# A fused attention and two-block feed-forward kernel: where four kinds of small steps run

## The chip, the cores and the metric

One core of a Trainium2 chip runs the whole program. The metric is the device time of one execution in microseconds (us). TensorE multiplies matrices into PSUM banks; VectorE, ScalarE and GpSimd do the elementwise work, each taking its instructions in a fixed order; SyncE (SP) issues the DMAs, in order too. VectorE is DVE in the rows, ScalarE ACT, GpSimd POOL, TensorE PE (PEld: its weight loads).

## The reference, cut to what matters

```python
def _attn_ref(q, k, v, g_q, g_k):              # q, k, v: (4, 12, 448, 64) float32
    def rmsnorm(x, g):
        rms = np.sqrt(np.mean(x * x, axis=-1, keepdims=True) + 1e-06)
        return x / rms * g
    q_n, k_n = rmsnorm(q, g_q), rmsnorm(k, g_k)
    scores = (1.0 / np.sqrt(64)) * np.matmul(q_n, k_n.transpose(0, 1, 3, 2))
    attn = np.exp(scores - np.max(scores, axis=-1, keepdims=True))
    attn = attn / (np.sum(attn, axis=-1, keepdims=True) + 1e-09)
    return np.matmul(attn, v).astype(np.float32)

x = attention output as 1792 x 768
x = (((x @ w1) * (x @ w2)) @ w3) @ w_out        # 768 -> 1024 -> 1024 -> 768
h = x @ w_in                                     # 768 -> 2048
return (h * np.clip(h + 3.0, 0.0, 6.0) / 6.0) @ w_out2
```

The attention inputs are float32. The six weight matrices are float64: they are scaled by a numpy float64 scalar.

## The kernel before, in words

All products with float32 accuracy are made of fp32r operands split into a high and a low part (`mm3`, lines 79 to 82: three matmuls per product). The low part is the source less the high part, made by a subtraction: of the weights and keys on GpSimd (`ws`, `woh`, `w`, `wis`, `wos`, `K`), of the query on VectorE (`qlo`).

The program has two large stages in time. In the first, 24 pairs of heads (NP = 24) go through attention, each in 8 steps: four 112-row blocks (NC = 4) of either head. A step t makes a score tile on TensorE (`score`, lines 536 and 537: query high and low part stacked on 128 partitions, against the key's high and low parts), scales it and takes its row maximum on VectorE (`scale_max`, L543), negates that maximum (`negate`, L550, one column of the 16-column tile `mx`), and takes the exponential on ScalarE one step later (`expo`, L555, with the negated maximum as bias and the row sum as second result). Eight steps later the probabilities are transposed on TensorE (L562), split by ScalarE (`thi`, L571) and VectorE (`tlo`, L581) and multiplied with V. The score tiles go through two PSUM banks.

Around it, a table of tasks (`at`, `tasks`, with the shifts of `SHIFT`) places the preparation of the next pairs by step: `qhi` at 8i, `qlo` at 8i+1, `ksplit` at 8i+6 (L516 on ScalarE, L517 on GpSimd), `load_q` and `load_k` of the pair after that, and for every second pair the norms of two pairs at once: squares (`ssq`, L436), sums (`ssum`, L442), then `rms1` and `rms2`, six small instructions on a 112 x 32 tile on VectorE (L448, L460 to L466) with a logarithm and an exponential on ScalarE between them. The query source tile `qr` has a single buffer, so its next load waits until the last reader is done. `xout` (L639, GpSimd) multiplies the attention output by the reciprocal row sums, which come back through DRAM as a broadcast.

Between the attention steps, `fill` puts matmuls of the feed-forward chain: first W' = w3 @ w_out (`wprime`), then, for each of four batches, w1 and w2 and W' (`layer1`, `layer2`). `Prep` converts the weights ahead of that: `convert` makes float32 bit patterns out of float64 words held as pairs of int32. Per weight tile, ScalarE scales the high word as a float (L135), VectorE shifts the low word right by 29 bits (L136), and two VectorE instructions join sign, exponent and mantissa (L138, L141).

In the second large stage the last block runs: its weights are converted by `conv_w` (the same `convert` on 128 x 768 tiles, two raw buffers `wr`; 13 of 32 before the stage's loop, 19 inside the first of its four rounds), split by `split` (L799 ScalarE, L800 GpSimd), and 36 matmuls per 128 columns of width follow, with the activation on ScalarE and VectorE (L871 to L876).

The order of instructions on an engine is made when the program is built: a planner takes them in the order of the program text and lets a later one go ahead where, by its own costs, the earlier one would not be ready.

Of the kernel before, what the change touches and what calls it, by code (L numbers as in the profile page):

```python
# [12 lines left out]
F32 = mybir.dt.float32  # L13
F32R = mybir.dt.float32r
I32 = mybir.dt.int32
SIGN = -(1 << 31)
AF = mybir.ActivationFunctionType
ALU = mybir.AluOpType
# [4 lines left out]
B, H, S, D = 4, 12, 448, 64  # L23
HP = H // 2
NP = B * HP
P = 128
# [20 lines left out]
def fused_kernel(ctx: ExitStack, tc: tile.TileContext, nat, qT, kT, vin, gq, gk,  # L47
                 w12, w3t, wo, win, wo2, outT):
    nc = tc.nc
# [15 lines left out]
    G = gs[:, 2:3]  # L65
# [3 lines left out]
    def fetch(pool, src, n, tag, bufs=2):  # L69
# [4 lines left out]
        else:  # L74
            r = pool.tile([P, n, 2], I32, tag=tag, bufs=bufs, name=tag)
            dma(r, src.bitcast(I32).rearrange("p (n t) -> p n t", t=2))
        return r
# [9 lines left out]
    def dma(out, src):  # L87
        return nc.sync.dma_start(out, src)
# [13 lines left out]
    def run_tasks():  # L102
        for fn, a in tasks.pop(now[0], ()):
            fn(*a)
# [24 lines left out]
    def convert(w, r):  # L129

        hi, lo = r[:, :, 1], r[:, :, 0]
        f = hi.bitcast(F32)
        nc.scalar.activation(f, f, AF.Copy, scale=2.0 ** -112)  # L135
        nc.vector.tensor_single_scalar(lo, lo, 29, op=ALU.logical_shift_right)  # L136
        yield 0.7
        nc.vector.scalar_tensor_tensor(out=lo, in0=hi, scalar=SIGN, in1=lo,  # L138
                                       op0=ALU.bitwise_and, op1=ALU.bitwise_or)
        yield 0.9  # L140
        nc.vector.scalar_tensor_tensor(out=w, in0=hi, scalar=3, in1=lo,  # L141
                                       op0=ALU.logical_shift_left, op1=ALU.bitwise_or)
        yield 0.9
# [258 lines left out]
    T = {}  # L402
    anchors = {}

    def attention(ap, rate):
# [10 lines left out]
                    dma(T["nat", i], nat[i].rearrange("p a b d -> p (a b) d"))  # L416

        def load_q(i):
            T["qr", i] = ap.tile([P, 2, S], F32, tag="qr", bufs=1, name="qr")
            dma(T["qr", i], qT[i])  # L420

        def load_k(i):
            T["kr", i] = ap.tile([P, 2, S], F32, tag="kr", bufs=1, name="kr")
# [14 lines left out]
        def ssum(i, g):  # L438
            x = T.pop(("nat", i))
            if i == g[0]:  # L440
                T["ss", g[0]] = ap.tile([CP, 2, len(g), 2 * NC], F32, tag="ss", bufs=2, name="ss")
            nc.vector.reduce_sum(T["ss", g[0]][:, :, i - g[0], :],  # L442
                                 x.rearrange("p (a b) d -> p a b d", a=2), axis=AX.X)

        def rms1(g):
            w = 16 * len(g)
            v = T["ss", g[0]].rearrange("p a b c -> p (a b c)")
            nc.vector.tensor_scalar(v, v, 1.0 / D, 1e-6, op0=ALU.mult, op1=ALU.add)  # L448
            y = ap.tile([CP, w], F32, tag="ry", bufs=2, name="ry")
            nc.scalar.activation(y, v, AF.Ln)  # L450
            nc.scalar.activation(y, y, AF.Exp, scale=-0.5)
            T["ry", g[0]] = y

        def rms2(g):
            n = len(g)
            w = 16 * n
            v = T.pop(("ss", g[0])).rearrange("p a b c -> p (a b c)")
            y = T.pop(("ry", g[0]))
            t = ap.tile([CP, w], F32, tag="rt", bufs=2, name="rt")
            nc.vector.tensor_mul(t, y, y)  # L460
            nc.vector.tensor_mul(t, t, v)
            nc.vector.tensor_scalar(t, t, -0.5, 1.5, op0=ALU.mult, op1=ALU.add)
            r = ap.tile([CP, w], F32, tag="rr", bufs=2, name="rr")
            nc.vector.tensor_mul(r, y, t)
            rq = ap.tile([CP, n, 8], F32, tag="rq", bufs=3, name="rq")
            nc.vector.tensor_scalar_mul(rq, r[:, : 8 * n].rearrange("p (a b) -> p a b", b=8), 0.125)  # L466
            for i in g:
                T["rq", i] = rq[:, i - g[0], :]
            T["rr", g[0]] = r
# [32 lines left out]

        def qhi(i):
            T["Q", i] = q = ap.tile([P, 2, S], F32R, tag="Q", bufs=2, name="Q")
            nc.scalar.activation(q, T["qr", i], AF.Copy, scale=G)

        def qlo(i):
            a = slice(64, 128)
            q = T["Q", i]
            nc.vector.scalar_tensor_tensor(out=q[a], in0=T["qr", i][a], scalar=G[a, :], in1=q[a],  # L510
                                           op0=ALU.mult, op1=ALU.subtract)

        def ksplit(i):
            k1, k2 = T["K", i] = [ap.tile([P, 2, S], F32R, tag=f"K{z}", bufs=2, name="K") for z in range(2)]
# [12 lines left out]
        def score(i, s):  # L527
            j, c = divmod(s, NC)
            if s == 0:
                T["PP", i] = ap.tile([CP, NC, 2 * S], F32, tag="PP", bufs=2, name="PP")  # L530
                T["m", i] = ap.tile([CP, 16], F32, tag="mx", bufs=2, name="mx")
                T["sum", i] = ap.tile([CP, 8], F32, tag="sum", bufs=2, name="sum")
            k1, k2 = T["K", i]
            ps = bank("s")
            qs = T["Q", i][:, j, c * CP : c * CP + CP]
            nc.tensor.matmul(ps[:CP, :S], qs, k1[:, j, :], start=True, stop=False)  # L536
            anchors[8 * i + s] = [nc.tensor.matmul(ps[:CP, :S], qs, k2[:, j, :], start=False, stop=True)]  # L537
            return ps
# [8 lines left out]

        def negate(i, s):
            m = T["m", i]
            nc.vector.tensor_scalar_mul(m[:, 8 + s : 9 + s], m[:, s : s + 1], -1.0)  # L550

        def expo(i, s):
            j, c = divmod(s, NC)
            v = T["PP", i][:, c, j * S : j * S + S]
            anchors[8 * i + s].append(nc.scalar.activation(  # L555
                v, v, AF.Exp, bias=T["m", i][:, 8 + s : 9 + s], accum_out=T["sum", i][:, s : s + 1]))
# [124 lines left out]
        for i in range(NP):  # L681
            t = 8 * i
            n = i + 1
# [9 lines left out]
            if i % 2 == 0 and i + 2 < NP:  # L693
                g = groups[i + 2]
# [19 lines left out]
            if i % 2 == 0 and i + 2 < NP:  # L714
                g = groups[i + 2]
# [5 lines left out]
        t = -1  # L721
        while t < 8 * NP + 22 or xs_ready:
            t += 1
            if t == 4:
                first.close()
            now[0] = t
            live = t < 8 * NP
            ps = score(*divmod(t, 8)) if live else None
            if 0 < t <= 8 * NP:
                expo(*divmod(t - 1, 8))  # L730
            u = t - LG
            if 0 <= u < 8 * NP and u % 8 < 7:
                trans(*divmod(u, 8))
            if 0 <= u - 1 < 8 * NP and (u - 1) % 8 < 7:
                tlo(*divmod(u - 1, 8))
            if live:
                scale_max(t // 8, t % 8, ps)
                negate(*divmod(t, 8))
            if 0 <= u < 8 * NP and u % 8 < 7:
                thi(*divmod(u, 8))  # L740
            if 0 <= u - 2 < 8 * NP and (u - 2) % 8 < 7:
                pv(*divmod(u - 2, 8))
            with ExitStack() as es:
                for a in anchors.get(t - (3 if "pool" in L else 2), ()):
                    es.enter_context(tc.issue_after(a.ins))
                fill(*rate(t))
            run_tasks()
            if "pool" in L:
                xnext()
# [37 lines left out]
    def conv_w(q):  # L787
# [4 lines left out]
        else:  # L792
            for _ in convert(wf[q].bitcast(I32), r):
                pass
# [10 lines left out]
    step, q = 0, 0  # L805
# [33 lines left out]
    for b, t in enumerate(order):  # L839
        acc = None  # L840
        for m in range(M2):
# [26 lines left out]
            if acc is None:  # L868
# [4 lines left out]
                                           op0=ALU.min, op1=ALU.mult)  # L873
            g = lp.tile([P, 2, S], F32R, tag="g", bufs=2, name="g")
# [57 lines left out]
```

## Time and profile before

| what | value |
|---|---|
| timed runs | 1273.02 us median of 3 (1271.57 to 1277.7) |
| profiled execution | 1276.18 us, of which 1274.3 us span from first to last instruction |
| granted TensorE clock, mean | 0.968 |
| TensorE busy | 1183.1 us, 93% |
| VectorE busy | 795.1 us, 62% |
| ScalarE busy | 678.8 us, 53% |
| GpSimd busy | 463.6 us, 36% |
| DMA moved | 203.72 MB |

The busy time of an engine is a share of the whole span; a stage in which another engine sets the pace shows only in a table by stretch. [...]

### The profile page before, as it was taken

What the parts mean: (1) busy time and instruction counts of PE and PEld (TensorE: products, weight loads), DVE (VectorE), ACT (ScalarE), POOL (GpSimd) and SP (SyncE); (2) the same over time, 40 slices, a digit from 0 to 9 for tenths busy, and PEclk for the clock granted to TensorE, in tenths of its full rate; (3) what the DMA queues carried; (4) which work ended last, traced back from release to release, by engine and by line L of the source; (5) the groups of instructions that cost most, each with busy time, mean ns of one, the idle gap of its engine ahead of it and who ended that gap; (6) DMA issues with size and microseconds to landing.
All of it is one profiled execution on the core that took longest, in us unless ns stands there. A gap on an engine that the chain in (4) does not pass through costs nothing.

```text
span 1274.3 us, 16884 instructions
## 1 busy us (share of the span) xinstructions
PE 1183.1 (93%) x5868; PEld 1033.9 (81%) x5868; DVE 795.1 (62%) x1524; ACT 678.8 (53%) x1305; POOL 463.6 (36%) x292
## 2 busy tenths in 40 slices
PE   3587998888889999999999999889999999999998
PEld 2355987667668999999998998778999999999997
DVE  6989789989993578768643446994433343343332
ACT  5887667866783566766642223444533353344332
POOL 4334324624443112222111003445454454545542
PEclk9698998989999999999999999899999999999999
DMA  7898664666688666676349983450100020001001
GB/s 248 253 256 243 202 193 167 194 229 228 211 274 306 209 217 199 235 225 220 134 163 382 348 323 113 158 173 25 60 28 1 1 87 1 1 1 44 1 1 44
DMA packets 64693, 203.72 MB, mean 160 GB/s; under 512 B 8544, under 2 KB 25440, under 8 KB 64608
## 3 DMA queue, kind: packets, MB, share of 16 engines
q1 hardware_dynamic: 64608, 202.65, 48.2%
q8 instruction: 46, 0.75, 0.2%
q14 instruction: 39, 0.32, 0.1%
HBM read 173.93 MB, written 28.68 MB: 159 GB/s over the span
## 4 chain that ended last, share of the span: by engine, by line
PE 67%; DMA 11%; DVE 10%; issue 5%; ACT 3%; POOL 2%; SPq 1%; DVEq 0%; POOLq 0%; ACTq 0%
PE bank L80 8%; PE bank L82 8%; PE bank L81 8%; PE acc L81 6%; PE acc L82 6%; PE acc L80 5%; PE h L80 5%; PE h L81 5%; PE h L82 5%; PE bank L562 3%; DMA raw<-in_w_dram 2%; DVE wf L141 2%; DMA wr<-in_wo_dram 2%; PE bank L536 2%; PE bank L537 2%
## 5 line engine op out<-in xcount | busy, mean ns | idle before, releaser
L800 POOL TENSOR_TENSOR wis<-wf,wis 128x768 fp32r<-128x768 f32 x63 | 119.8, 1902 | 234.1 <-ACT wis L799 234.1
L872 DVE SCALAR_TENSOR_TENSOR u<-u,h 128x448 f32<-128x448 f32 x64 | 39.5, 618 | 217.3 <-ACT u L871 217.3
L800 POOL TENSOR_TENSOR wos<-wf,wos 128x768 fp32r<-128x768 f32 x64 | 119.0, 1860 | 103.6 <-ACT wos L799 103.6
L80 PE MATMUL bank<-xhl,ws 128*128 128x448 f32 x384 | 145.1, 378 | 7.7 <-ACT ws L285 6.3
L543 DVE CUSTOM_DVE_ANT_0 PP<-bank,rb,rq 112x448 f32<-112x448 f32 x192 | 129.1, 677 | 31.9 <-PE bank L537 27.4
L82 PE MATMUL bank<-xhl,ws 128*128 128x448 f32 x384 | 143.9, 375 | 4.9 <-POOL ws L287 4.9
L81 PE MATMUL acc<-g,wos 128*128 128x448 f32 x384 | 144.3, 376 | 3.8 <-DVE g L876 3.7
L555 ACT ACTIVATE PP<-PP,mx 112x448 f32<-112x448 f32 x192 | 127.4, 664 | 37.4 <-DVE mx L550 34.2
L80 PE MATMUL acc<-g,wos 128*128 128x448 f32 x384 | 138.5, 371 | 5.5 <-ACT g L875 5.5
L82 PE MATMUL acc<-g,wos 128*128 128x448 f32 x384 | 143.2, 373 | 0.0
L81 PE MATMUL bank<-xhl,ws 128*128 128x448 f32 x384 | 142.5, 371 | 0.1
L80 PE MATMUL h<-x2h,wis 128*128 128x448 f32 x378 | 139.0, 368 | 0.0
L81 PE MATMUL h<-x2h,wis 128*128 128x448 f32 x378 | 138.9, 368 | 0.0
L82 PE MATMUL h<-x2h,wis 128*128 128x448 f32 x378 | 137.5, 364 | 0.4 <-POOL wis L800 0.4
L876 DVE TENSOR_TENSOR g<-u,g 128x448 fp32r<-128x448 f32 x64 | 97.9, 1529 | 33.6 <-ACT g L875 33.6
L871 ACT ACTIVATE u<-h,half 128x448 f32<-128x448 f32 x64 | 40.4, 631 | 143.2 <-PE h L82 143.2
L536 PE MATMUL bank<-K,Q 128*112 128x448 f32 x192 | 78.3, 409 | 37.5 <-DVE mx L543 25.0
L562 PE MATMUL bank<-ident,PP 112*128 112x112 f32 x672 | 97.0, 267 | 11.8 <-DVE xl L581 10.2
L562 PEld LDWEIGHTS bank<-ident,PP 112*128 112x128 f32 x672 | 80.5, 145 | 33.8 <-DVE xl L581 13.3
L571 ACT ACTIVATE xh<-bank 128x448 fp32r<-128x448 f32 (+1 forms) x156 | 83.0, 537 | 43.3 <-PE bank L562 38.4
L581 DVE TENSOR_TENSOR xl<-bank,xh 128x448 fp32r<-128x448 f32 x142 | 87.1, 615 | 25.5 <-ACT xh L571 23.8
L799 ACT ACTIVATE wos<-wf 128x768 fp32r<-128x768 f32 x64 | 54.1, 846 | 86.9 <-PE acc L82 86.7
(126 smaller groups left out, 2763.5 us busy)
## 6 DMA issues: line engine op xcount, KB each, us to landing
ws<-w12d SPq DMA_DIRECT2D x48, 768.0 KB, 5.1
ws<-wpd SPq DMA_DIRECT2D x32, 768.0 KB, 4.2
raw<-in_w_dram SPq DMA_DIRECT2D x32, 384.0 KB, 4.3
w12d<-ws SPq DMA_DIRECT2D x16, 768.0 KB, 6.0
wr<-in_win_dram SPq DMA_DIRECT2D x16, 768.0 KB, 4.5
wr<-in_wo_dram SPq DMA_DIRECT2D x16, 768.0 KB, 6.6
nat<-in_nat_dram SPq DMA_DIRECT2D x24, 448.0 KB, 5.9
qr<-in_qT_dram SPq DMA_DIRECT2D x24, 448.0 KB, 6.4
```

What stands on the lines that cost most here:

```text
L80: nc.tensor.matmul(ps, lh, rh, start=first, stop=False)
L81: nc.tensor.matmul(ps, lh, rl, start=False, stop=False)
L82: return nc.tensor.matmul(ps, ll, rh, start=False, stop=last)
L536: nc.tensor.matmul(ps[:CP, :S], qs, k1[:, j, :], start=True, stop=False)
L543: anchors[8 * i + s].append(nc.vector.tensor_tensor_reduce(out=T["PP", i][:, c, sl], in0=ps[:CP, :S], in1=T["rb", i][:, sl], op0=ALU.mult, ...
L555: anchors[8 * i + s].append(nc.scalar.activation(v, v, AF.Exp, bias=T["m", i][:, 8 + s : 9 + s], accum_out=T["sum", i][:, s : s + 1]))
L562: nc.tensor.transpose(ps[:, c * CP : c * CP + CP], src[:, c, kb * P : kb * P + P], ident[:CP, :CP])
L571: nc.scalar.activation(hi, ps, AF.Copy)
L581: nc.vector.tensor_sub(lo, ps, hi)
L799: nc.scalar.activation(t[:, 0, :], wf[q], AF.Copy)
L800: nc.gpsimd.tensor_sub(t[:, 1, :], wf[q], t[:, 0, :])
L876: nc.vector.tensor_sub(g[:, 1, :], u, g[:, 0, :])
```

## The change

Five edits. The shift of the low word becomes a ScalarE activation: it reads the upper 16 bits of the low word as an unsigned integer, multiplies by 2^-13, adds 2^-14 - 0.5 and writes an int32, which rounds to the top three bits. The norm steps of all groups but the first go to GpSimd. The query is loaded on 64 partitions instead of twice on 128; ScalarE scales it in place and copies it as the high part in a second instruction, and GpSimd subtracts to get the low part. Maxima are negated two columns at a time on odd steps. The exponential is placed one step later.

```diff
@@ convert
         hi, lo = r[:, :, 1], r[:, :, 0]
+        top = r.bitcast(U16).rearrange("p n (t s) -> p n t s", s=2)[:, :, 0, 1]
         f = hi.bitcast(F32)
         nc.scalar.activation(f, f, AF.Copy, scale=2.0 ** -112)
-        nc.vector.tensor_single_scalar(lo, lo, 29, op=ALU.logical_shift_right)
+        nc.scalar.activation(lo, top, AF.Copy, scale=2.0 ** -13, bias=2.0 ** -14 - 0.5)
@@ load_q
-            T["qr", i] = ap.tile([P, 2, S], F32, tag="qr", bufs=1, name="qr")
-            dma(T["qr", i], qT[i])
+            T["qr", i] = ap.tile([D, 2, S], F32, tag="qr", bufs=1, name="qr")
+            dma(T["qr", i], qT[i][:D])
@@ rms1, rms2
+        def eng(g):
+            return nc.gpsimd if g[0] else nc.vector
-            nc.vector.tensor_scalar(v, v, 1.0 / D, 1e-6, op0=ALU.mult, op1=ALU.add)
+            eng(g).tensor_scalar(v, v, 1.0 / D, 1e-6, op0=ALU.mult, op1=ALU.add)
...
-            nc.vector.tensor_mul(t, y, y)
+            eng(g).tensor_mul(t, y, y)
...
@@ qhi, qlo
-            nc.scalar.activation(q, T["qr", i], AF.Copy, scale=G)
+            qr = T["qr", i]
+            nc.scalar.activation(qr, qr, AF.Copy, scale=G[:D, :])
+            nc.scalar.activation(q[:D], qr, AF.Copy)
-            nc.vector.scalar_tensor_tensor(out=q[a], in0=T["qr", i][a], scalar=G[a, :], in1=q[a],
-                                           op0=ALU.mult, op1=ALU.subtract)
+            nc.gpsimd.tensor_sub(q[D:], T["qr", i], q[:D])
@@ negate
-            nc.vector.tensor_scalar_mul(m[:, 8 + s : 9 + s], m[:, s : s + 1], -1.0)
+            if s % 2:
+                nc.vector.tensor_scalar_mul(m[:, 7 + s : 9 + s], m[:, s - 1 : s + 1], -1.0)
@@ the step loop
-            if 0 < t <= 8 * NP:
-                expo(*divmod(t - 1, 8))
+            if 1 < t <= 8 * NP + 1:
+                expo(*divmod(t - 2, 8))
```

## Rows read from the trace of the kernel before

**Rows 1.** The page, part 1: busy us, share of the span, instructions.
```profile
PE 1183.1 (93%) x5868; PEld 1033.9 (81%) x5868; DVE 795.1 (62%) x1524; ACT 678.8 (53%) x1305; POOL 463.6 (36%) x292
```

**Rows 2.** Busy time of each engine by stretch; the first line names the columns.
```profile
core 0: us, PE busy (x) PEld busy (x) DVE busy (x) ACT busy (x) POOL busy (x), PEclk, DMA share, GB/s
0.00:400.00 400.00, 323.51 (x1553) 255.61 (x1554) 349.99 (x833) 287.25 (x619) 165.56 (x123) 0.91 0.73 228
400.00:650.00 250.00, 250.00 (x1383) 226.67 (x1382) 164.57 (x405) 151.31 (x326) 49.19 (x34) 1.00 0.63 207
...
785.00:870.00 85.00, 76.10 (x339) 65.66 (x337) 79.77 (x70) 37.81 (x54) 40.06 (x20) 0.94 0.40 140
```

**Rows 3.** The same view for 40 to 100 us, the same columns.
```profile
40.00:100.00 60.00, 44.67 (x186) 26.79 (x184) 56.32 (x133) 48.22 (x99) 24.74 (x18) 0.83 0.88 238
```

**Rows 4.** Waits of TensorE, 0 to 400 us: total us, times, longest.
```profile
PE bank L536 <- DVE mx L543: 25.0, 16, 5.8
...
PE bank L562 <- DVE xl L581: 10.2, 8, 3.3
```

**Rows 5.** Groups by line, VectorE, 0 to 400 us: count, busy us, mean ns, idle.
```profile
L510 DVE SCALAR_TENSOR_TENSOR Q<-qr,gs,Q 64x896 fp32r<-64x896 f32 x16 | 26.3, 1646 | 3.8 <-ACT Q L505 3.4
...
L136 DVE TENSOR_SCALAR raw<-raw 128x384 int32<-128x384 int32 x48 | 23.0, 480 | 10.5 <-DMA raw<-in_w_dram 5.6 <-DMA raw<-in_wo_dram 4.7
...
L550 DVE TENSOR_SCALAR mx<-mx 112x1 f32<-112x1 f32 x116 | 16.2, 143 | 0.5
...
L136 DVE TENSOR_SCALAR raw<-raw 128x512 int32<-128x512 int32 x16 | 11.8, 736 | 1.6 <-DMA raw<-in_w3t_dram 1.6
...
L460 DVE TENSOR_TENSOR rt<-ry 112x32 f32<-112x32 f32 x12 | 7.1, 590 | 0.1
L634 DVE TENSOR_SCALAR sum<-sum 112x8 f32<-112x8 f32 x14 | 5.4, 384 | 0.0
...
L464 DVE TENSOR_TENSOR rr<-ry,rt 112x32 f32<-112x32 f32 x10 | 2.3, 229 | 0.0
```

**Rows 6.** The same view, ScalarE and GpSimd.
```profile
L517 POOL TENSOR_TENSOR K<-kr,K 128x896 fp32r<-128x896 f32 x16 | 35.5, 2216 | 33.6 <-ACT K L516 26.7 <-DMA nat<-in_nat_dram 6.8
...
L135 ACT ACTIVATE raw<-raw 128x384 f32<-128x384 f32 x48 | 26.6, 556 | 13.9 <-DMA raw<-in_w_dram 11.5 <-DMA raw<-in_wo_dram 2.2
...
L505 ACT ACTIVATE Q<-qr,gs 128x896 fp32r<-128x896 f32 x16 | 16.6, 1034 | 1.9 <-DMA qr<-in_qT_dram 1.9
...
L639 POOL TENSOR_TENSOR xs<-xs,rsb 128x448 f32<-128x448 f32 x12 | 14.4, 1202 | 27.4 <-DMA rsb<-rsd 19.4 <-DVE raw L136 2.7 <-ACT PP L555 2.1
...
L135 ACT ACTIVATE raw<-raw 128x512 f32<-128x512 f32 x16 | 10.7, 670 | 3.8 <-DMA raw<-in_w3t_dram 3.7
```

**Rows 7.** Timeline, 817.9 to 827.6 us: start, us, engine, line, operation, tiles.
```profile
817.96 0.33 SPq L88 DMA_DIRECT2D wr<-in_win_dram  x1
...
822.39 0.55 DVE L136 TENSOR_SCALAR wr<-wr 128x768 int32<-128x768 int32 x1
...
822.44 0.94 ACT L135 ACTIVATE wr<-wr 128x768 f32<-128x768 f32 x1 [3.30 <-DMA wr<-in_win_dram]
...
823.28 0.56 ACT L875 ACTIVATE g<-u 128x448 fp32r<-128x448 f32 x1
...
823.41 0.96 DVE L138 SCALAR_TENSOR_TENSOR wr<-wr 128x768 int32<-128x768 int32 x1 [0.47 <-ACT wr L135]
...
824.83 2.60 DVE L141 SCALAR_TENSOR_TENSOR wf<-wr 128x768 int32<-128x768 int32 x1
...
827.49 0.33 SPq L88 DMA_DIRECT2D wr<-in_win_dram  x1
```

**Rows 8.** Stretch 40 to 100 us, L136 alone: busy (count), clock, DMA.
```profile
40.00:100.00 60.00, 6.51 (x13) 0.83 0.88 238
```

**Rows 9.** L550 and L634: count, duration ns least/median/most, first and last start.
```profile
L550 DVE TENSOR_SCALAR mx<-mx x192: 130/147/156, 22.4 to 640.4; 112x1 f32<-112x1 f32 x192
...
L634 DVE TENSOR_SCALAR sum<-sum x24: 151/172/1244, 44.9 to 641.4; 112x8 f32<-112x8 f32 x24
```

More of the change, by code (lines that the diff above doesn't have):

```diff
@@ L15 @@
 I32 = mybir.dt.int32
+U16 = mybir.dt.uint16
 SIGN = -(1 << 31)
@@ L459, in rms2 @@
             t = ap.tile([CP, w], F32, tag="rt", bufs=2, name="rt")
-            nc.vector.tensor_mul(t, y, y)
-            nc.vector.tensor_mul(t, t, v)
-            nc.vector.tensor_scalar(t, t, -0.5, 1.5, op0=ALU.mult, op1=ALU.add)
+            eng(g).tensor_mul(t, y, y)
+            eng(g).tensor_mul(t, t, v)
+            eng(g).tensor_scalar(t, t, -0.5, 1.5, op0=ALU.mult, op1=ALU.add)
             r = ap.tile([CP, w], F32, tag="rr", bufs=2, name="rr")
-            nc.vector.tensor_mul(r, y, t)
+            eng(g).tensor_mul(r, y, t)
             rq = ap.tile([CP, n, 8], F32, tag="rq", bufs=3, name="rq")
-            nc.vector.tensor_scalar_mul(rq, r[:, : 8 * n].rearrange("p (a b) -> p a b", b=8), 0.125)
+            eng(g).tensor_scalar_mul(rq, r[:, : 8 * n].rearrange("p (a b) -> p a b", b=8), 0.125)
             for i in g:
@@ L504, in qhi @@
             T["Q", i] = q = ap.tile([P, 2, S], F32R, tag="Q", bufs=2, name="Q")
-            nc.scalar.activation(q, T["qr", i], AF.Copy, scale=G)
+            qr = T["qr", i]
+            nc.scalar.activation(qr, qr, AF.Copy, scale=G[:D, :])
+            nc.scalar.activation(q[:D], qr, AF.Copy)
         def qlo(i):
-            a = slice(64, 128)
             q = T["Q", i]
-            nc.vector.scalar_tensor_tensor(out=q[a], in0=T["qr", i][a], scalar=G[a, :], in1=q[a],
-                                           op0=ALU.mult, op1=ALU.subtract)
+            nc.gpsimd.tensor_sub(q[D:], T["qr", i], q[:D])
         def ksplit(i):
```

## The prediction, made before the changed kernel was run

> **What bounds the kernel now.** I read the busy table first [rows 1]: TensorE 93%, VectorE 62%, ScalarE 53%, GpSimd 36%. It suggests TensorE, but these are averages over stages with different limits, so the second view is the same table by stretch [rows 2]. From 400 to 650 us TensorE is busy all the time, at full clock, and gets through 1383 matmuls, 5.53 per us. In the first 400 us it gets through 1553, for which that rate would need 281 us: 119 us are lost there, and that is the most that anything can win in this stretch. There VectorE is busy 350.0 of 400 us (0.875), ScalarE 287.3 (0.72), GpSimd 165.6 (0.41); in the densest part, 40 to 100 us, VectorE 56.3 of 60 (0.94) and ScalarE 48.2 (0.80) [rows 3]. The third view, TensorE's waits in these 400 us, names VectorE again: 25.0 us for the scaled maxima of L543, which give back the score bank, and 10.2 us for the low parts of L581 [rows 4]. So up to 400 us the bound is VectorE's queue; after that it is TensorE, except for one stretch: from 785 to 870 us TensorE loses 9 us, its clock is 0.94, and VectorE is busy 79.8 of 85 us [rows 2]. What is won or lost before 400 us reaches the end one to one, since TensorE has no slack to swallow it afterwards.
>
> **What VectorE loses, first 400 us.** The query low parts L510: 16 instructions, 26.3 us. The shift L136: 48 of 480 ns and 16 of 736 ns, 34.8 us. The norm steps: six groups of 10 to 12 small instructions, 24.1 us, of which L460 (7.1) is the largest and L464 (2.3) the smallest; the first of twelve pairs of heads stays on VectorE, so 22.1 us go. The negations L550: 116 of 143 ns, 16.2 us; half as many at the same price save 8.1 [rows 5]. Together 91 us: VectorE falls from 350 to 259 us.
>
> **What ScalarE gains.** The shift becomes an activation of the form of L135: same tile, same stride of 8 bytes, so I price it by L135's rows, 26.6 + 10.7 us. The query's second pass over 64 partitions has as many columns as L505, 16.6 us [rows 6]. That is 53.9 us of durations. Consecutive activations overlap: L135 starts at 822.44, lasts 0.94, and the next starts at 823.28 [rows 7], 0.10 early. Over 80 new ones this takes 8 us off: ScalarE goes from 287 to 333 us and becomes the fullest engine of the stage.
>
> **What GpSimd gains.** The query low part has the columns of L517, 2216 ns: 16 of them, 35.5 us. No norm step on GpSimd is in the trace. A line through L639 (448 columns, 1202 ns) and L517 (896 columns) [rows 6] puts 32 columns at 0.3 us; bounds are 0.2 (VectorE's own small price, L464, 229 ns) and 1.2 (L639). I take 0.3, about 65 instructions in the stretch: 20 us. GpSimd goes to 221 us, 0.55. What hides it: the low part is emitted at step 8i+1 and its first matmul at step 8i+8; 116 steps took 400 us (the count of L550, [rows 5]), 3.4 us each, so 24 us of cover for 2.2 us of work. The norm results run pairs ahead. If the cover is gone, 16 times 2.2 us, 35 us, is the price. Behind a waiting low part stand on GpSimd the key low parts, the split of V and the weight low parts; on SP the next load of q, which needs its single buffer back, and every load issued behind it.
>
> **The sum of this stage.** If ScalarE at 333 us is packed as tightly as VectorE was (0.875), the stage takes 381 us, 19 less. In 40 to 100 us nothing is won: 13 of the shifts there [rows 8] and two query passes bring ScalarE from 48 to about 56 of 60 us, where VectorE was. I take 3 us off for that: −16. Bounds: packed to VectorE's best 0.94 it is 354 us, −46; packed as ScalarE is now (0.72), 463 us, +63. I stand near the middle value because ScalarE's idle time is largely waiting on the VectorE queue that gets lighter, and because the exponential, emitted one step later, finds its maximum ready.
>
> **The negation in pairs.** The trace has a warning. L550, one element wide, took 130, 147 and at most 156 ns in 192 instructions; L634, the same operation eight wide, took 151, 172 and up to 1244 ns [rows 9], with a mean of 384 in the first 400 us [rows 5]. Something holds the wider one and never the narrow one. The change makes the narrow one two wide. The price is between zero and L634's excess over L550, 58 times 0.24 us, 14 us of VectorE; I take half as VectorE time, 7 us, and zero on the path, since 266 us is still far under ScalarE's 333.
> [...]
>
> **The weight conversion from 785 to 870 us.** One loop sets the pace there, visible in [rows 7]: the load of `wr` is issued at 817.96, lands for L135 at 822.44, L138 starts at 823.41 when L135 is done, L141 ends at 827.43, and the next load of that buffer goes out at 827.49: 9.53 us, about 9 such rounds in the stretch. L136 costs this loop nothing, it runs at 822.39 beside L135. Its successor runs after L135 on ScalarE and holds L138 0.84 us longer (822.44 to 823.28). TensorE's own 36 matmuls need less than the loop. Six of the nine rounds are paced by it, the first ones having their loads in hand: +5. Bounds: +8 if all nine are, and −10 if VectorE's queue, relieved of two L136 of 0.55 us per round, was the true limit.
>
> **Loads of q.** 448 KB become 224 KB, 16 times in the stretch. DMA was no releaser of TensorE there; bounds 0 and −4, I take −1.
>
> Sum: −16 + 5 − 1 = −12. The profiled execution took 1276.2 us (span 1274.3), so 1264; it lies 3.2 above the median of the timed runs, 1273.0, so the forecast is 1261 us. The likeliest case has a range of its own from 1245 to 1269.
>
> **Rivals.**
> 1. ScalarE cannot be filled. It is the engine that everything else releases: its order is fixed, and now the logarithm of the norm waits behind GpSimd (2.2 us key parts, and L639, which kept GpSimd 19.4 us waiting for its broadcast [rows 6]), and conversions need two activations where one did. Its best stretch so far is 0.80 [rows 3]. At 0.80 the stage takes 416 us: +16 + 5 − 1, 1293 us. It decides at 333/400 = 0.83: packed below that, the stage is slower than before. For: the added wait and the 0.72. Against: it idles on VectorE's results. Chance 0.20.
> 2. The paired negation is held behind GpSimd on the path: scaled maxima queue behind it, TensorE waits for the bank. 14 us come back: 1275 us, no change. For: L634. Against: VectorE's slack. Chance 0.13.
> 3. VectorE was the whole problem and ScalarE packs to 0.94 except for the densest part, with the clock returning as TensorE runs denser: half to two thirds of −46, near −30 + 4: 1247 us. For: [rows 4] lists hardly a wait on ScalarE of that size. Chance 0.14.
> The edits doing nothing because the removed work was hidden anyway is part of 2: it would show as a first stage of 400 us with an emptier VectorE.
> The forecast itself: 0.53.
>
> **How the numbers follow.** A change under 0.5% (6.4 us) can't be told from none here. Faster than that: 0.47 of the forecast's 0.53 and all of rival 3, 0.61. Within: 0.06 of the forecast, 0.09 of rival 2, 0.03 of rival 1, 0.18. Slower: 0.17 of rival 1 and 0.04 of rival 2, 0.21. The range goes from 1238, half of rival 3, to 1288, just short of rival 1.
>
> **What would show it.** In the first 400 us of work (116 steps): VectorE near 0.7, ScalarE near 0.87, fewer waits of TensorE on L543; L550's successor with a maximum far over 156 ns tells rival 2. Between 785 and 870 us: a round of 10.3 us instead of 9.5. The forecast is wrong if the point where TensorE becomes saturated does not move ahead by 10 us or more, or if ScalarE's waits on GpSimd grow by more than VectorE's shrink.

## The result and the profile after

The changed kernel took 1286.55 us (median of 4 runs, 1286.45 to 1288.95) against 1273.49 for the kernel before on the same chip: ratio 1.0105, 95% interval [1.0087, 1.0124]. It is 13 us slower; the forecast was 12 us faster. The profiled execution has a span of 1284.7 us.

The page's first part (busy us, share, instructions), to be read beside [rows 1]:

```profile
PE 1183.0 (92%) x5868; PEld 1034.1 (80%) x5868; DVE 729.0 (57%) x1242; ACT 747.0 (58%) x1425; POOL 530.2 (41%) x382
```

Work did move as the change says: VectorE lost 66 us over the run, ScalarE gained 68, GpSimd 67. TensorE does the same work in the same busy time, so the 10 us more of span are 10 us more in which it stands. The first two stretches of [rows 2] and the 85 us from the last stage's first activation, same columns:

```profile
0.00:400.00 400.00, 314.17 (x1486) 245.91 (x1487) 310.86 (x624) 320.72 (x687) 205.72 (x195) 0.89 0.69 210
400.00:650.00 250.00, 250.00 (x1375) 226.70 (x1374) 151.23 (x348) 155.29 (x335) 74.73 (x53) 1.00 0.64 207
...
798.40:883.40 85.00, 75.09 (x350) 64.57 (x351) 64.28 (x53) 52.33 (x74) 41.10 (x20) 1.00 0.41 140
```

The whole loss lies in the first line. TensorE gets through 1486 matmuls in place of 1553 and its granted clock (PEclk, a share of full speed) is 0.89 in place of 0.91; 314.2 x 0.89 against 323.5 x 0.91 is 15 us less of full-speed work. Some 9 us of that are TensorE standing longer (85.8 us against 76.5), the other 6 the lower granted clock. From 400 to 650 us it is saturated in both kernels, so the lag is carried: the last stage's first activation comes at 798.4 us where it came at 784.6 (+13.8). In the last stage 3.4 us are won back: from that first activation to the last 475.3 us, before 478.7. And no engine is full in the first 400 us: VectorE 0.78, ScalarE 0.80, GpSimd 0.51, TensorE 0.79. They wait for one another.

TensorE's waits in that stretch (line waited for, total us, times, longest), beside [rows 4]:

```profile
PE bank L541 <- POOL Q L516: 21.3, 2, 15.7
PE bank L568 <- DVE xl L587: 15.5, 10, 4.7
PE bank L541 <- DVE mx L548: 13.3, 16, 2.0
```

The wait for the scaled maxima was halved (25.0 to 13.3), as intended. The wait for the low parts grew from 10.2 to 15.5, and TensorE's first score now waits for GpSimd's low part, until 15.7 us where before it started at 11.4; the second of these two waits, 5.7 us, is at 54 us.

VectorE's groups by line and form in the first 400 us (busy us, mean ns), beside [rows 5]:

```profile
L143 DVE SCALAR_TENSOR_TENSOR raw<-raw 128x384 int32<-128x384 int32 x48 | 40.4, 843 | 0.5
L140 DVE SCALAR_TENSOR_TENSOR raw<-raw 128x384 int32<-128x384 int32 x48 | 40.0, 836 | 11.6 <-ACT raw L138 10.7 <-POOL K L522 0.9
...
L556 DVE TENSOR_SCALAR mx<-mx 112x2 f32<-112x2 f32 x57 | 23.1, 406 | 0.3
...
L640 DVE TENSOR_SCALAR sum<-sum 112x8 f32<-112x8 f32 x14 | 10.3, 738 | 4.3 <-ACT PP L561 4.2
```

Half as many negations take 23.1 us where 116 narrow ones took 16.2. The two joins of the 384-column tiles cost 836 and 843 ns where they cost 685 and 716, and L640 costs 738 where it cost 384. So of the 91 us that were taken off VectorE a good part returned as longer durations of what stayed: summed over all its groups, 403 us became 346, −57 and not −91. The difference is mostly the negation (23.1 us where 8.1 were forecast, +15.0), the joins of both widths (91.6 to 108.9, +17.3) and L640 (+4.9). They are longer only beside GpSimd: of the 128 joins, the 74 that overlap a two-source instruction of GpSimd took 1046 ns on average, the other 54 took 586 and at most 694 (before: 61 of 855 and 67 of 588). Of the 57 negations, 21 overlap one and took 831 ns on average, the other 36 at most 170; of the 14 L640, ten overlap one and took 969 on average, the other four at most 172.

ScalarE's new groups, same view, beside [rows 6]:

```profile
L138 ACT ACTIVATE raw<-raw 128x384 int32<-128x384 uint16 x48 | 26.6, 555 | 0.0
L511 ACT ACTIVATE qr<-qr,gs 64x896 f32<-64x896 f32 x17 | 17.9, 1053 | 15.7 <-DMA qr<-in_qT_dram 15.7
L512 ACT ACTIVATE Q<-qr 64x896 fp32r<-64x896 f32 x16 | 15.2, 950 | 0.0
```

The shift on ScalarE costs what was forecast (555 ns, L135 had 556). The query's scale pass is new in one thing: ScalarE stands before it for the load, 15.7 us here and 25.9 over all 24 pairs; before it did so once, for 1.9.

### The profile page after: what moved, and what is told of

It is laid out like the page before. It is cut to its first block, busy times and chain, and to the rows that moved or that the text cites. A ratio compares the mean times of both kernels' runs of the same rounds, so it can differ in the third digit from the quotient of the medians.

```text
span 1284.7 us, 16794 instructions
## 1 busy us (share of the span) xinstructions
PE 1183.0 (92%) x5868; PEld 1034.1 (80%) x5868; DVE 729.0 (57%) x1242; ACT 747.0 (58%) x1425; POOL 530.2 (41%) x382
## 4 chain that ended last, share of the span: by engine, by line
PE 65%; DMA 12%; ACT 9%; DVE 6%; issue 4%; POOL 3%; SPq 1%; ACTq 0%; POOLq 0%; DVEq 0%
PE bank L81 8%; PE bank L83 8%; PE bank L82 8%; PE acc L81 5%; PE acc L82 5%; PE acc L83 5%; PE h L81 5%; PE h L82 5%; PE h L83 5%; PE bank L568 3%; DMA wr<-in_win_dram 3%; ACT PP L561 2%; PE bank L541 2%; DMA wpd<-wst 2%; DMA nat<-in_nat_dram 2%
## 5 line engine op out<-in xcount | busy, mean ns | idle before, releaser
L82 PE MATMUL acc<-g,wos 128*128 128x448 f32 x384 | 141.7, 369 | 2.5 <-DVE g L882 2.5
L81 PE MATMUL acc<-g,wos 128*128 128x448 f32 x384 | 137.2, 370 | 5.0 <-ACT g L881 4.9
L83 PE MATMUL acc<-g,wos 128*128 128x448 f32 x384 | 141.2, 368 | 0.0
L882 DVE TENSOR_TENSOR g<-u,g 128x448 fp32r<-128x448 f32 x64 | 99.3, 1552 | 35.5 <-ACT g L881 35.5
L568 PE MATMUL bank<-ident,PP 112*128 112x112 f32 x672 | 100.3, 274 | 18.2 <-DVE xl L587 15.5
```

What stands on the lines that cost most here:

```text
L81: nc.tensor.matmul(ps, lh, rh, start=first, stop=False)
L82: nc.tensor.matmul(ps, lh, rl, start=False, stop=False)
L83: return nc.tensor.matmul(ps, ll, rh, start=False, stop=last)
L568: nc.tensor.transpose(ps[:, c * CP : c * CP + CP], src[:, c, kb * P : kb * P + P], ident[:CP, :CP])
L882: nc.vector.tensor_sub(g[:, 1, :], u, g[:, 0, :])
```

## The experiments

All kernels differ from the kernel before or from the change in what is named. Ratios are to the kernel before on the same chip.

**One edit at a time.** First the parts alone. The theories then were S, that ScalarE is too full to be filled further (rival 1), Q, that the query's low part reaches TensorE late, and L, that the paired negation is held behind GpSimd (rival 2).

```
a_shift: before + shift of the low words on ScalarE
a_norm:  before + norm steps on GpSimd
a_query: before + half load, two ScalarE passes, GpSimd low part
a_neg:   before + maxima negated in pairs, exponential a step later
```

> The kernel before with the shift of the low words on ScalarE, nothing else. Theory S (ScalarE is the engine that got too full): most of the loss of 13 us is here, +6 to +12 us, and in the first 400 us VectorE waits for the new activation. Theory Q (the query's low part reaches TensorE late): within 4 us of before. Theory L (the paired negation is held behind GpSimd): within 4 us or faster, since VectorE loses 35 us of work.

> The kernel before with only the norm steps on GpSimd. All three theories: faster or the same, -8 to 0 us, since 22 us of small VectorE instructions go; slower by over 4 us would mean that the logarithm on ScalarE waits behind GpSimd.

> The kernel before with only the query edit (half load, two passes on ScalarE, low part on GpSimd). Theory Q: +8 to +12 us, of which 4 to 5 us are at the start (first score matmul at 15.7 instead of 11.4 us). Theory S: 0 to +5. Theory L: faster by up to 6 us, since VectorE loses 26 us.

> The kernel before with only the negation in pairs and the exponential one step later. Theory L: +4 to +10 us, and the two-wide negation takes up to 2 us where the one-wide took 156 ns at most. Theories S and Q: -6 to +2 us.

Measured: a_shift 1269.66 us, 0.998 [0.9964, 0.9997]; a_norm 1278.77, 1.0039 [1.0017, 1.006]; a_query 1287.85, 1.0128 [1.0103, 1.0152]; a_neg 1287.92, 1.0122 [1.0096, 1.0147]. The parts sum to 1.027, the whole is 1.0105: they don't add. a_query and a_neg lose more than any theory said (16 and 15 us), and a_norm, which all three had as no slower, loses 5. That isn't the logarithm waiting behind GpSimd, for ScalarE stood before it for only 1.9 us in the first 400 us. Theory S falls with a_shift, whose window of the first 400 us reads:

```profile
0.00:400.00 400.00, 318.71 (x1575) 257.54 (x1576) 327.37 (x761) 310.81 (x678) 159.78 (x122) 0.92 0.73 233
```

ScalarE is at 310.8 us (0.78), 24 more than before, and TensorE gets through more matmuls (1575), not fewer.

**Is it GpSimd's hold?** Theory P is that GpSimd's instructions hold up VectorE's, one for one. In a_query there is such a place. Its timeline from 123.7 us (start, us, engine, line, operation, tiles):

```profile
123.68 2.10 POOL L511 TENSOR_TENSOR Q<-qr,Q 64x896 fp32r<-64x896 f32 x1
124.06 2.28 DVE L138 SCALAR_TENSOR_TENSOR raw<-raw 128x512 int32<-128x512 int32 x1
125.86 2.42 POOL L517 TENSOR_TENSOR K<-kr,K 128x896 fp32r<-128x896 f32 x1
126.37 2.46 DVE L141 SCALAR_TENSOR_TENSOR raw<-raw 128x512 int32<-128x512 int32 x1
128.25 5.52 POOL L203 TENSOR_TENSOR w<-raw,w 128x512 fp32r<-128x512 f32 x4
128.76 1.27 DVE L460 TENSOR_TENSOR rt<-ry 112x32 f32<-112x32 f32 x1
```

GpSimd works back to back, and each of these VectorE instructions takes about as long as a GpSimd instruction beside it (the four of L203 take 1.4 us each). To take that away, the low part went to VectorE, for all pairs (b_q_dve) or for the first pair only (b_q_first). Theory O, in some expectations from here on, is that the new order of instructions costs, whatever the edit is.

```
-            nc.gpsimd.tensor_sub(q[D:], T["qr", i], q[:D])
+            nc.vector.tensor_sub(q[D:], T["qr", i], q[:D])                        # b_q_dve
+            (nc.gpsimd if i else nc.vector).tensor_sub(q[D:], T["qr", i], q[:D])  # b_q_first
```

> The kernel before with the query edit, but the first pair's low part on VectorE. Theory Q (the query's low part is late): the start comes back, 4 to 5 us, and another 2 to 5 at the third pair if the order allows: 1278 to 1284 us. Theory O: 1283 to 1290 us.

> The kernel before with the query edit, but every low part subtracted on VectorE as before. [...] Theory A (the second activation and the load cost): 1283 to 1288 us.

Measured: b_q_first 1286.44 us, 1.0108 [1.0088, 1.0128]; b_q_dve 1292.0, 1.0147 [1.0123, 1.0171]. Without GpSimd the query edit is no better: by P most of the 15 us would have come back, and none did, and theory A, that the second activation and the load cost, is exceeded too. But VectorE's order in b_q_dve is another one than in a_query (see below), so a smaller price of the hold isn't excluded. b_q_first lies in theory O's range. TensorE's waits in b_q_dve, 0 to 400 us:

```profile
PE bank L562 <- DVE xl L581: 20.7, 10, 3.5
PE bank L536 <- DVE mx L543: 18.6, 20, 2.1
PE bank L536 <- DVE Q L511: 16.4, 3, 14.4
```

The start (a wait of 14.4 us) is as late with VectorE's low part as with GpSimd's (14.5); GpSimd is not what makes it late. (d_qone below, with one ScalarE pass, has its first score at 11.2 us.)

**The pair of negations.** The same two columns negated by another form of instruction, in a_neg (b_negr, whose order on all engines is that of a_neg) and in the whole change (c_negr). And the change without its pair negation (c_noneg).

```
-  nc.vector.tensor_scalar_mul(m[:, 7 + s : 9 + s], m[:, s - 1 : s + 1], -1.0)
+  nc.vector.reduce_max(m[:, 7 + s : 9 + s], m[:, s - 1 : s + 1].rearrange("p (a b) -> p a b", b=1),
+                       axis=AX.X, negate=True)
```

> The kernel before with only the maxima negated in pairs and the exponential one step later, as in the run that did this alone (1.2% slower), but the pair is negated by a reduction over one element with the sign turned, in the same place of every engine's order. Theory L (the two-wide multiplication is held behind GpSimd instructions): most of the 15 us come back, 1270 to 1277 us, and the reduction never takes over 0.3 us. Theory O (it is the new order of instructions that costs, whatever the negation is): no change, 1283 to 1290 us.

> The changed kernel with the same reduction in place of the two-wide multiplication, the order otherwise the same. Theory L: 5 to 12 us less than the changed kernel, 1274 to 1281 us. Theory O: 1284 to 1289 us.

> The changed kernel with the maxima negated one at a time and the exponential at its old step. Alone this edit cost 15 us; beside the others the paired negation's wait is partly covered (the reduction in its place gave back 2 us): 1278 to 1285 us. Over 1286 us would mean that it costs nothing there.

Measured: b_negr 1279.08 us, 1.0044 [1.0026, 1.0062]; c_negr 1284.33, 1.0091 [1.0068, 1.0113]; c_noneg 1282.04, 1.0068 [1.0042, 1.0094]. The group in a_neg, then the one in b_negr (0 to 400 us):

```profile
L551 DVE TENSOR_SCALAR mx<-mx 112x2 f32<-112x2 f32 x57 | 25.3, 445 | 0.2
```

```profile
L551 DVE TENSOR_REDUCE mx<-mx 112x2 f32<-112x2 f32 x58 | 8.4, 145 | 0.2
```

Same columns, same order, a third of the time: alone, the hold costs 17 us of VectorE's time and about 10 us of the run (0.0078 of 1273). b_negr lies between the ranges of theories L and O; the 5.6 us that stay are not this hold. In the whole change, again in the same order, the hold is worth about 2 us, with intervals that overlap, as theory O had it; leaving the pairing out altogether gives 5.

**Which edit carries the whole.** The change without its query edit (c_noq), and the shift on ScalarE for the last stage's 128 x 768 tiles only (s_big):

```
c_noq: qr, load_q, qhi, qlo as in the kernel before, the rest as changed
s_big: before, and in convert:
+        if r.shape[1] < DM:
+            nc.vector.tensor_single_scalar(lo, lo, 29, op=ALU.logical_shift_right)
+        else:
+            nc.scalar.activation(lo, top, AF.Copy, scale=2.0 ** -13, bias=2.0 ** -14 - 0.5)
```

> The changed kernel with the query as it was before. Theory P: the query is the largest part, 1274 to 1280 us. If the parts only fill the same gaps, 1281 to 1287 us.

> The kernel before with the shift on ScalarE for the 128 x 768 tiles of the last block alone; the attention stage keeps its order. The step as predicted (the second activation lengthens the load loop): +3 to +5 us, a round near 10.3 us. Against it (VectorE's queue sets the round, and two shifts leave it): -3 to -5 us, a round near 8.7 us.

Measured: c_noq 1273.6 us, 1.0002 [0.9978, 1.0027]; s_big 1269.19, 0.9966 [0.9943, 0.9988]. So without its query edit the change costs nothing. s_big and a_shift are the only versions faster than the kernel before, by 4.3 and 2.5 us. The stretch 785 to 870 us of s_big:

```profile
785.00:870.00 85.00, 75.53 (x353) 64.86 (x352) 66.00 (x53) 51.24 (x71) 42.29 (x21) 1.00 0.40 139
```

VectorE is at 66.0 us where it was at 79.8 [rows 2], and the stage from its first to its last activation takes 475.1 us (before 478.7). The gain is as the run's second alternative said (3 to 5 us); its round near 8.7 us is not there, the rounds of the load loop are 9.8 us on average.

**What in the query edit?** Theory H: the load of half the partitions, behind which ScalarE stands in its fixed order. In a_query, ScalarE's waits from 0 to 650 us:

```profile
ACT qr L506 <- DMA qr<-in_qT_dram: 22.3, 12, 3.9
```

Theory A: the second ScalarE pass and the longer chain. d_qfull keeps the passes and loads all 128 partitions; d_qone keeps the half load with one pass and VectorE's low part; d_qbuf2 is the query edit with two load buffers; d_afull is the whole change with the full load.

```
d_qfull, d_afull:
+  T["qr", i] = ap.tile([P, 2, S], F32, tag="qr", bufs=1, name="qr"); dma(T["qr", i], qT[i])
d_qone:
+  nc.scalar.activation(q[:D], T["qr", i], AF.Copy, scale=G[:D, :])
+  nc.vector.scalar_tensor_tensor(out=q[D:], in0=T["qr", i], scalar=G[:D, :], in1=q[:D], ...)
d_qbuf2:
-  ... tag="qr", bufs=1      tag="xs", bufs=8
+  ... tag="qr", bufs=2      tag="xs", bufs=6
```

> The kernel before with the query edit (two ScalarE passes, low part on GpSimd), but the load again of all 128 partitions; the upper 64 are loaded and not used. Theory H (the load of half the partitions takes as long as the whole one, and the first ScalarE pass is put close behind it, so that ScalarE stands for the load in its fixed order: 22 us in 12 waits): at most 5 of those waits, and 1272 to 1278 us. Theory A (the second ScalarE pass and the longer chain to the low part): 1284 to 1292 us, with the PE waits on xl near 30 us as with the half load.

> The kernel before with the half load alone: one ScalarE pass of 64 partitions with the scale, the low part by VectorE's scalar_tensor_tensor as before. Theory H: the half load does the harm, 1283 to 1290 us, and ScalarE waits for the query load over 15 us. Theory A: within 3 us of the kernel before, 1271 to 1277 us.

> The kernel before with the query edit and two buffers of the loaded queries in place of one (attention outputs kept in 6 buffers in place of 8, to make room). Theory H: the load can be issued a pair earlier, the ScalarE waits for it go below 5 us and the time to 1272 to 1279 us. Theory A: the waits go, the time stays at 1284 to 1292 us.

> The whole change with the load again of all 128 partitions (the upper 64 not used). Theory H: near the change without its query edit, 1272 to 1277 us. Theory A: no better than the change, 1284 to 1289 us.

Measured: d_qfull 1295.23 us, 1.0166 [1.0136, 1.0196]; d_qone 1281.99, 1.007 [1.0048, 1.0092]; d_qbuf2 1294.16, 1.0164 [1.0136, 1.0192]; d_afull 1276.23, 1.0027 [1.0008, 1.0046]. Both theories miss: H has the time of d_afull alone, and there ScalarE still stands 21.9 us for the load; A has none; and with two buffers the waits don't go (25.3 us in d_qbuf2). The full load makes the query edit alone no better (1295 against 1288) and mends the whole change by 10 us: one and the same edit, with opposite signs. And d_qone is slower by 9 us with nothing in it that costs an engine more. Its query groups, 0 to 400 us:

```profile
L505 ACT ACTIVATE Q<-qr,gs 64x896 fp32r<-64x896 f32 x16 | 16.6, 1036 | 2.6 <-DVE ss L660 1.7 <-DMA qr<-in_qT_dram 0.9
```

```profile
L509 DVE SCALAR_TENSOR_TENSOR Q<-qr,gs,Q 64x896 fp32r<-64x896 f32 x16 | 24.2, 1513 | 2.9 <-ACT Q L505 2.3
```

ScalarE's pass is as long as before (1034 ns [rows 6]), VectorE's shorter (1513 against 1646 [rows 5]), the wait for the load 0.9 us. Each engine has as many instructions as in the kernel before. What did change is their order: the planner, given a load of half the size, dealt the instructions of every engine anew (when the sequences of tile names are aligned with those before, the similarity is 0.65 on VectorE and 0.74 on ScalarE, where 1 is the same; it is 0.52 on VectorE between a_query and b_q_dve). A new order is no loss in itself: a_shift has 0.54 and 0.58 and is faster.

**Order alone.** Theory O, in a sharper form: what an edit costs here is mostly what the newly dealt order makes of the waits. Two runs keep every instruction of the change and only place the query split elsewhere in the table of tasks, e_later all of it, e_earlier its two ScalarE passes:

```
-SHIFT = {'ssum': -1, ...
+SHIFT = {'qhi': 4, 'qlo': 4, 'ssum': -1, ...      # e_later
+SHIFT = {'qhi': -2, 'ssum': -1, ...               # e_earlier
```

> The whole change with the query split (both ScalarE passes and GpSimd's subtraction) placed 4 steps later in the table of tasks; the same instructions on every engine in another order. Theory O (what the edits cost is what the re-dealt fixed order makes of the waits, not a price of the operations): the time moves by 4 us or more either way from the change's 1286, and the matmuls that TensorE makes in the first 400 us move with it (1486 in the change, 1553 before). Theory W (ScalarE's standing for the query load is the price: 25.9 us in 18 waits): those waits fall below 8 us and the time to 1272 to 1278 us. If the operations themselves cost it: within 3 us of 1286.

> The whole change with the first part of the query split placed 2 steps earlier; the same instructions on every engine in another order. Theory O: the time moves by 4 us or more either way from 1286, with the matmuls of the first 400 us. Theory W: ScalarE meets the load still sooner behind its issue, waits over 26 us, 1287 to 1294 us. If the operations themselves cost it: within 3 us of 1286.

Measured: e_later 1278.07 us, 1.0054 [1.0031, 1.0078]; e_earlier 1277.04, 1.0031 [1.001, 1.0053]; the change had 1.0105 [1.0087, 1.0124]. With the same instructions, 7 to 9 us of its 13 are gone, whichever way the split is moved. The first 400 us of e_later, then of e_earlier:

```profile
0.00:400.00 400.00, 323.23 (x1544) 256.93 (x1545) 322.83 (x633) 325.50 (x699) 213.85 (x201) 0.90 0.70 218
```

```profile
0.00:400.00 400.00, 315.09 (x1541) 250.82 (x1542) 308.55 (x609) 315.61 (x676) 206.77 (x197) 0.93 0.71 220
```

ScalarE's busy time is above (325.5) or below (315.6) that of the change (320.7), and TensorE has 55 to 58 matmuls more. Theory W, that ScalarE's wait for the load is the price, falls: it is 19.4 us in e_later, nowhere near the 8 it needed, and 17.2 in e_earlier, where it should have grown.

The two rows differ in how the matmuls came back. In e_later TensorE stands 9 us less than in the change (76.8 against 85.8 us) at nearly the same granted clock. In e_earlier it stands as long as in the change (84.9 us), and the granted clock is 0.93 in place of 0.89. Over all timed runs the mean clock is 0.965 for the change, 0.970 for e_earlier and 0.969 for e_later. So the order is worth 7 to 9 us, but shorter waits are seen in e_later only; why the clock is higher in e_earlier isn't shown.

A null edit was tried too: GpSimd clears the row sums of one pair of heads at each of its steps, so that this kernel leaves out part of that pair's sums.

```
+            if i == 8:
+                nc.gpsimd.memset(T["sum", i], 0.0)      # b_null2, inside score
```

> The kernel before with one added instruction that does nothing useful: the row sums of pair 8 are set to zero on GpSimd before they are written. It is there because the planner deals out another order for it. Theory O: +5 to +15 us, as the single edits that move work. Theories L and Q: within 3 us of before, since nothing is added to any engine.

Measured: 1278.94 us, 1.0045 [1.0027, 1.0063]. It is not a clean null, since it adds waits between engines at the eight steps of that pair; it says no more than that.

**All of them in one table** (from the window view of the first 400 us and the start of the last stage's first activation; the ratio is of medians, the rest of one profiled execution each, which for c_noq lies 7.2 us above its own median, for b_null2 7.8 below, and for the others within 3.2):

```
            ratio   matmuls   VectorE  ScalarE  first activation
d_qbuf2    1.0164    1437      337.8    282.3     804.5
d_qfull    1.0166    1459      345.0    289.8     805.1
a_query    1.0128    1479      346.3    288.1     796.2
change     1.0105    1486      310.9    320.7     798.4
c_negr     1.0091    1486      297.1    319.4     798.3
b_q_dve    1.0147    1491      351.6    291.9     801.6
a_neg      1.0122    1495      358.4    279.5     795.0
b_q_first  1.0108    1497      350.6    294.1     795.5
c_noneg    1.0068    1498      297.1    319.4     794.7
d_qone     1.0070    1508      345.6    280.3     791.8
c_noq      1.0002    1509      324.7    305.9     791.2
b_negr     1.0044    1530      353.6    284.1     787.9
a_norm     1.0039    1531      354.7    287.8     788.9
d_afull    1.0027    1540      310.2    327.7     786.8
e_earlier  1.0031    1541      308.6    315.6     786.1
e_later    1.0054    1544      322.8    325.5     786.7
before     1        1553      350.0    287.3     784.6
s_big      0.9966    1567      351.6    287.8     782.7
a_shift    0.9980    1575      327.4    310.8     778.4
b_null2    1.0045    1583      361.0    295.9     779.4
```

Read down the columns: leaving c_noq and b_null2 aside, the time goes roughly with the matmuls that TensorE gets through in the first 400 us, as it must where TensorE is saturated afterwards. VectorE's busy time doesn't order the rows (c_negr at 297 us and b_q_first at 351 have 1.0091 and 1.0108, d_afull at 310 and a_norm at 355 have 1.0027 and 1.0039), nor does ScalarE's (282 at the top, 311 at the bottom).

**What a dealt order does.** Two places of the change where TensorE stood nearly 5 us. The timeline from 283 us:

```profile
283.17 1.13 POOL L645 TENSOR_TENSOR xs<-xs,rsb 128x448 f32<-128x448 f32 x1 [4.01 <-DMA rsb<-rsd]
...
284.57 0.25 POOL L466 TENSOR_TENSOR rt<-rt,ss 112x32 f32<-112x32 f32 x1
...
284.86 2.35 DVE L444 TENSOR_REDUCE ss<-nat 112x16 f32<-112x1024 f32 x2 [4.28 <-POOL rt L466]
...
287.65 0.62 DVE L587 TENSOR_TENSOR xl<-bank,xh 128x448 fp32r<-128x448 f32 x1
...
288.33 1.01 PE L568 MATMUL bank<-ident,PP 112*128 112x112 f32 x4 [4.75 <-DVE xl L587]
```

Read it from the last line up. TensorE waits for a low part; that part stands on VectorE behind a row sum, L444; L444 waits for a norm step, L466, which has moved to GpSimd; and L466 stands on GpSimd behind the output scaling L645, which waits 4.0 us for its broadcast from DRAM. Before, the norm step stood on VectorE and nothing of VectorE's waited for GpSimd in these 400 us. From 280.6 to 284.9 us VectorE stands idle, with work behind L444 in its order. The second place, from 384 us:

```profile
384.74 2.07 POOL L516 TENSOR_TENSOR Q<-qr,Q 64x896 fp32r<-64x896 f32 x1
384.90 2.33 DVE L140 SCALAR_TENSOR_TENSOR raw<-raw 128x384 int32<-128x384 int32 x1
...
387.26 1.26 DVE L143 SCALAR_TENSOR_TENSOR raw<-raw 128x384 int32<-128x384 int32 x1
...
388.87 0.62 DVE L589 TENSOR_TENSOR xh<-bank,xh 64x448 fp32r<-64x448 f32 x1
...
389.54 0.74 PE L611 MATMUL bank<-xh,vo 128*128 128x448 f32 x1 [4.81 <-DVE xh L589]
```

Here weight conversions stand on VectorE ahead of the low part, and the first of them runs 2.33 us beside GpSimd's 2.07 us query subtraction. In e_later the waits of the first place are shorter, here its group of L444 and its wait for low parts (0 to 400 us):

```profile
L444 DVE TENSOR_REDUCE ss<-nat 112x16 f32<-112x1024 f32 x22 | 26.3, 1212 | 5.8 <-ACT nat L438 5.3 <-POOL rt L466 0.3
```

```profile
PE bank L568 <- DVE xl L587: 6.5, 6, 2.2
```

VectorE's wait for L466 goes from 6.2 to 0.3 us and TensorE's for low parts from 15.5 to 6.5, with the same instructions on both engines. The wait of the second place, for L589, is 0.5 us there.

## Why the prediction was wrong, step by step

**What bounds the kernel: half right.** That the first 400 us decide and that the rest passes the lag on unchanged held (+13.8 at the first activation of the last stage, nothing lost after it). "The bound is VectorE's queue" was wrong as a statement on busy time: c_negr empties VectorE to 297 us and is 1% slower. What the other engines gain was near its forecast: GpSimd's low parts took 35.5 us as said, its norm steps 22 for 20, ScalarE's activations 555 ns for 556.

**The sum of this stage, −16: the step that failed.** It let an engine's busy time set the stage: ScalarE at 333 us, packed like VectorE, makes 381. ScalarE came out at 320.7 for 114 of the 116 steps, close to forecast, and packed to 0.80, so that the stage came out some 14 us longer and not 19 shorter. But fullness is not why, for e_later has ScalarE at 325.5 and loses half as much. In its place the runs show the order: the same instructions in two other orders are 7 to 9 us faster. The edit made new chains across engines with fixed orders, such as the low part at 288 us behind a row sum, a norm step and a broadcast. That such chains are the whole loss is argued from the two places (9.6 us of TensorE's standing), not shown; part of the 15 us is the lower granted clock, and what lowers it isn't shown either. Rival 1 had the packing (0.80), and its 1293 us are near the time, but not by its mechanism: a_shift adds 24 us to ScalarE and is faster, the same instructions pack ScalarE to 0.81 in e_later (and to 0.82 in d_afull, with the full load), and the logarithm that it saw waiting for GpSimd waited for nothing:

```profile
L455 ACT ACTIVATE ry<-ss 112x32 f32<-112x32 f32 x12 | 2.8, 235 | 0.0
```

What waited behind the norm steps and their broadcast was VectorE's row sum.

**What VectorE loses, 91 us: 57.** The removed instructions went; 34 us came back, as longer durations of those that stayed and now overlap GpSimd's (and 4 us for the first group's norm steps, priced at 2). The prediction counted GpSimd's 55 us as cover-only work and gave it no price on VectorE.

**The pair of negations, 7 us of VectorE and zero on the path: the size was off.** The warning of [rows 9] was read rightly: 146, 169 and up to 2161 ns, as L634 had shown. The traces show what the long ones stand beside: in the first 400 us of the kernel before, five of the 14 L634 overlap a two-source instruction of GpSimd and took 792 ns on average, the other nine at most 161; of the 57 pairs in the changed kernel 21 overlap one and took 831, the others at most 170. The reduction on the same two columns took 145 ns on average in b_negr, and at most 157, where a_neg has 445. The price is 15 us of VectorE's time, a little over the upper bound of 14, and about 10 us on the path when made alone, where zero was taken. In the whole change it is about 2 of the 13.

**The last stage, +5: wrong sign, −3.4.** The loop did become longer as forecast; loads of `wr` in the changed kernel (start, us, queue; every second one is of the same buffer):

```profile
810.23 0.33 SPq L89 DMA_DIRECT2D wr<-in_win_dram  x1
...
816.94 0.33 SPq L89 DMA_DIRECT2D wr<-in_wo_dram  x1
...
820.98 0.33 SPq L89 DMA_DIRECT2D wr<-in_win_dram  x1
...
827.17 0.33 SPq L89 DMA_DIRECT2D wr<-in_wo_dram  x1
```

These two rounds take 10.75 and 10.23 us, against 9.53 [rows 7] and a forecast of 10.3. All 13 of the loop take 8.2 to 11.4 us, 9.8 on average, where they took 9.5 before. Counted from the stage's first activation, the loop's last join ends 3.4 us later than before (87.9 against 84.5 us), and yet the stage ends 3.4 us sooner. So the loop did not pace TensorE. What most likely did is VectorE's queue, which the prediction kept only as its lower bound: in the same 85 us VectorE is at 64 in place of 80 us. TensorE stands no less there (9.9 against 8.5 us), at a granted clock of 1.00 in place of 0.94. But the clock alone isn't the reason: the stage takes 474.8 to 476.8 us in all nine kernels with the shift on ScalarE, also at 0.96 (a_shift), and 478.7 to 480.7 in all eleven without, also at 1.00 (b_null2).

**The query's cover, and the loads at −1.** The low part had its cover at most pairs, but not at the start, where nothing lies before it (4.2 us later at the first score), nor at the third pair, whose first score waits 5.7 us for it. Half the bytes landed little or no sooner (6.1 us in d_qbuf2, 7.0 in a_query, 6.4 before), and ScalarE, placed close behind the load, stood for it. That wait itself isn't the price (e_later); the order that came with the edit is.

**What stays open.** e_later and e_earlier keep 4 to 7 us of loss; the late start is of that size, and e_later keeps the wait of the third pair too (5.5 us), but no run removed either by itself with the order kept. Whether another order would let the lighter VectorE pay was not found, and why these orders and not others fall out well wasn't traced beyond the two places above. How much of the loss is the granted clock, and whether the order lowers it, was not tested.

## What to carry to other kernels

Here, where no engine was full (at most 0.80 of the first 400 us in the changed kernel) and a planner wrote each engine's order, the busy time that the edit moved didn't forecast the time: 57 us left VectorE there, and the run took 13 us longer. So count the chains that an edit makes across engines, what stands before each new wait and what stands behind it. Before an edit's time is called its price, deal the order anew with the same instructions; here that alone was worth 7 to 9 of 13 us. Where two kernels have the same order on every engine (a_neg and b_negr), the difference is a price. Moving work off VectorE to GpSimd gave less than the durations said, 57 us of 91, since what stayed on VectorE ran longer beside it.

## What the runs showed of the hardware that was not expected

- A load of 64 partitions (224 KB) took 7.0 us from issue to landing (median, a_query) and 6.1 in d_qbuf2, the one of 128 partitions (448 KB) 6.4 in the kernel before and 5.2 in d_afull; its issue took 0.48 us in place of 0.33.
- Negating two columns by `tensor_scalar` took 445 ns on average in a_neg, up to 2098 beside a two-source instruction of GpSimd and at most 169 elsewhere; by a reduction with negation 145 and at most 157.
- An activation that reads 16-bit words at a stride of 8 bytes and writes int32 took as long as one of float32 (555 and 558 ns for 384 columns in the changed kernel).
- Norm steps of 112 x 32 on GpSimd took 274 to 447 ns on average in the changed kernel, near the 0.3 us of the estimate.
- In the first 400 us of each of the twenty kernels, the joins on VectorE that no two-source instruction of GpSimd overlapped took 577 to 593 ns on average and at most 702; those that one did overlap took 830 to 1112 on average.
